# One matmul with doubled rows for the last 64 keys of a head, instead of two half-empty ones

## The chip, the cores and the metric

The kernel runs on one core of one Trainium2 chip. The number that counts is the device time of one execution in microseconds (us). The core has five engines, each with its own queue of instructions: PE (matrix multiply), DVE (vector), ACT (scalar and activation), POOL (GpSimd) and SP, which here only issues DMAs.

## The reference

All inputs are fp32. An attention with a threshold feeds two dense layers:

```
scores = 0.125 * q @ k.T            # 2 batches, 8 heads, 576 queries and keys, 64 dims
scores = where(scores >= rowmax - tau, scores, -1e9)
attn   = softmax(scores)
x      = (attn @ v), heads side by side          # 1152 tokens x 512
x      = max(x @ w1, x @ w2, x @ w3) @ w_out     # 512 -> 768 -> 512
out    = sum_e p[:, e] * (relu(x @ u1[e]) @ u2[e])   # 4 experts, 512 -> 1024 -> 512
```

The change concerns `attn @ v` alone, and of its 576 keys only the last 64 of each head.

## The kernel before, in words

**Precision.** Every fp32 operand is split into a high part (a copy rounded to the fp32r type that PE multiplies) and a low part (what is left, `x - high`), and PE adds up the products of the parts. For `attn @ v` the stationary operand is a tile of 128 columns, 64 columns of the high and 64 of the low values of one head; the moving operand is the weights, first their high part, then their low part. The two halves of the product's 128 rows are then added (`pvlo`, line 483, and line 485).

**Tiling of the attention.** Heads go in pairs, a "job"; there are 4 jobs for each batch. 576 keys are 4 chunks of 128 (`NC = 4`) and a remainder of 64 (`REM`). The queries of a pair are worked in steps: 4 chunks of 128 for each head, and one step for the 64 remaining queries of both heads (`st.h is None`), 9 steps in a job. A step forms scores on PE (`qk`, line 361), the row maximum on DVE (`peak`, 372), the exponential on ACT (`power`, 379), threshold and sum on DVE (`weigh`, 384), the scaling by one over the sum on POOL (`norm`, 391), the transposes on PE (`turn`, 401 and 404), and the split into high and low weights (`cut_hi`, `cut_lo`, 426 to 459).

**The remaining keys.** Both heads of a pair share one tile: head 0's 64 remaining keys are in partitions 0 to 63, head 1's in 64 to 127, so that one transpose (line 404, after every step of head 1 and after the step of the remaining queries) and one copy and one subtraction on all 128 partitions (`ar`, lines 438 and 459) serve both heads. The values `VR` hold zeros in the other head's partitions (the memset of line 292). For each head `gather` (line 474 on) then multiplies 4 chunks with high weights, the remainder with high weights, 4 chunks with low weights and the remainder with low weights: 10 matmuls, of 256 or of 320 columns.

**Stages.** In stage A the four jobs of batch 0 run alone; the order of its instructions on each engine comes from a list scheduler (`ORDER_A = ""`). In stage B the four jobs of batch 1 run between the matmuls of the dense layers for batch 0, and the order on PE, DVE, ACT and POOL is the order in which the program is written (`ORDER_B = "pdas"`). The issue order of SP's DMAs is the scheduler's in both. A third stage, without attention, works the dense layers for the rest of the tokens; its matmuls and those of stage B have line 1190. Their weights are split by ACT (line 711) and POOL (line 715), which the attention uses too.

**Loads.** Remaining values come with one DMA for a job (`vnrem`, line 175), on SP's queue in stage A and on ACT's queue in stage B. The stacked keys and queries that `qk` reads are made by DMAs from one part of the on-chip memory to another on SP's queue (`K`, lines 227 to 230, `QS`, line 243).

Of the kernel before, what the change touches and what calls it, by code (L numbers as in the profile page):

```python
# [22 lines left out]
def fused_kernel(ctx: ExitStack, tc: tile.TileContext, q, k, v, tau, w1, w2, w3, w_out, probs, m_w1, m_w2, out):  # L23
    nc = tc.nc
    B, H, S, D = q.shape
    NT, DM = out.shape
    DFF = w1.shape[1]
    E, _, F2 = m_w1.shape
    P = 128
    NPAIR = H // 2  # L30
    NC = S // P
    MAIN = NC * P
    REM = S - MAIN
# [61 lines left out]
    ident = cst.tile([P, P], F32, name="ident")  # L95
# [39 lines left out]
    at = {}  # L135
# [9 lines left out]
    def atile(shape, dt, tag):  # L145
        return at["pool"].tile(shape, dt, tag=tag, name=tag, bufs=at["bufs"].get(tag, 1))
# [4 lines left out]
    def load_job(job, names="qkv"):  # L151
        b, p = job.b, job.p
        for nm, src in (("q", q), ("k", k), ("v", v)):
            if nm not in names:
                continue
            heads = src[b, 2 * p:2 * p + 2]
            load = nc.scalar.dma_start if nm == "v" and b else nc.sync.dma_start
            main = heads[:, 0:MAIN, :].rearrange("h (p c) d -> p h c d", c=NC)
            if nm == "v":
                t = atile([P, 2, NC, D], F32, "vnat")  # L160
                load(out=t, in_=main)
            else:
                t = atile([P, NC, 2, D], F32, f"{nm}nat")
                for h in range(2):
                    nc.sync.dma_start(out=t[:, :, h, :], in_=main[:, h])
            if nm == "q":
                r = diagonal
                for h in range(2):
                    last = nc.sync.dma_start(out=r[h * REM:(h + 1) * REM, h * D:(h + 1) * D], in_=heads[h, MAIN:S, :])
            elif nm == "k":  # L170
                r = atile([REM, 2, D], F32, "knrem")
                last = nc.sync.dma_start(out=r, in_=heads[:, MAIN:S, :].rearrange("h r d -> r h d"))
            else:
                r = atile([P, D], F32, "vnrem")
                last = load(out=r, in_=heads[:, MAIN:S, :])
            job.raw[nm] = (t, r)
        return last

# [108 lines left out]

    def values(job, follower=None):
        V = atile([P, 2, NC, 2 * D], F32R, "V")
        if job.b == 0 or job.p == 0:  # L290
            at["VR"] = atile([P, 2, 2 * D], F32R, "VR")
            nc.gpsimd.memset(f32(at["VR"]), 0.0)
        VR = at["VR"]
        job.v = (V, VR)
        vt, vr = job.raw["v"]
        vn = vt
        nc.scalar.activation(out=V[:, :, :, 0:D], in_=vn, func=AF.Copy)
        yield
        nc.gpsimd.tensor_tensor(out=V[:, :, :, D:2 * D], in0=vn, in1=f32(V[:, :, :, 0:D]), op=ALU.subtract)
        rows = [slice(h * REM, (h + 1) * REM) for h in range(2)]  # L300
        for h, r in enumerate(rows):
            nc.scalar.activation(out=VR[r, h, 0:D], in_=vr[r, :], func=AF.Copy)
        yield
        for h, r in enumerate(rows):
            nc.gpsimd.tensor_tensor(out=VR[r, h, D:2 * D], in0=vr[r, :], in1=f32(VR[r, h, 0:D]), op=ALU.subtract)
        if follower:
            for _ in range(3):
                yield
            load_job(follower, "v")
# [77 lines left out]
    def norm(st, swift=False):  # L387
        em = views(st)[1]
        su, re = st.stat["sum"], st.stat["r"]
        nc.vector.reciprocal(out=re, in_=su)  # L390
        last = (nc.vector if swift else nc.gpsimd).tensor_scalar(out=em, in0=em, scalar1=re, scalar2=one, op0=ALU.mult, op1=ALU.mult)  # L391
        if st.h is None:
            nc.gpsimd.tensor_scalar(
                out=st.em[:, S:S + REM], in0=st.em[:, MAIN:S], scalar1=1.0, scalar2=1.0, op0=ALU.mult, op1=ALU.mult)
        return last

    def turn(st):
        st.t = ptile_at("T", [P, NC, P])
        off = (st.h or 0) * W
        for j in range(NC):  # L400
            last = nc.tensor.transpose(st.t[:, j, :], st.em[:, off + j * P:off + (j + 1) * P], ident)  # L401
        if st.h != 0:
            st.tm = ptile_at("U", [P, P])
            last = nc.tensor.transpose(st.tm, st.em[:, MAIN:MAIN + 2 * REM], ident)  # L404
        return last

    def pieces(st):
        grp = st.grp
        cols = slice(grp.nn, grp.n) if st.h is None else slice(st.ci * P, (st.ci + 1) * P)
        outs = []  # L410
        for h in range(2):
            if st.h in (h, None):
                if grp.am[h] is None:
                    grp.am[h] = [atile([P, NC, grp.n], F32R, "am") for _ in "hl"]
                src = slice(h * REM, (h + 1) * REM) if st.h is None else slice(0, P)
                outs.append((src, *(x[:, :, cols] for x in grp.am[h])))
        return cols, outs

    def rem_rows(st):
        if st.h == 0:  # L420
            return []
        return [slice(0, P)] if st.h == 1 else [slice(h * REM, (h + 1) * REM) for h in range(2)]

    def cut_hi(st, mode):

        st.mode = mode
        grp = st.grp
        cols, outs = pieces(st)
        if mode == "pool":
            st.copy = atile([P, NC, P], F32, "tcopy")  # L430
            nc.scalar.activation(out=st.copy, in_=st.t, func=AF.Copy)
        else:
            for src, hi, lo in outs:
                nc.scalar.activation(out=hi, in_=st.t[:, :, src], func=AF.Copy)  # L434
        for r in rem_rows(st):
            if not hasattr(grp, "ar"):
                grp.ar = [atile([P, grp.n], F32R, "ar") for _ in "hl"]
            nc.scalar.activation(out=grp.ar[0][r, cols], in_=st.tm[r, r], func=AF.Copy)

    def cut_lo(st):  # L440
        grp = st.grp
        cols, outs = pieces(st)
        if st.mode == "pe":
            t2 = ptile_at("T", [P, NC, P])
            off = st.h * W
            for j in range(NC):
                nc.tensor.matmul(
                    t2[:, j, :], lhsT=st.em[:, off + j * P:off + (j + 1) * P], rhs=ident, is_transpose=True, start=j == 0, stop=False)
        for src, hi, lo in outs:
            if st.mode == "pool":  # L450
# [14 lines left out]
    def gather(grp, swift=False):  # L465
# [7 lines left out]
        for h in range(2):  # L473
            pv = ptile_at("U", [P, n])
            terms = []
            for part in range(2):
                terms += [(V[:, h, j, :], grp.am[h][part][:, j, :]) for j in range(NC)]
                terms.append((VR[:, h, :], grp.ar[part]))
            for i, (l, r) in enumerate(terms):
                at["valued"] = nc.tensor.matmul(pv, lhsT=l, rhs=r, start=i == 0, stop=i == len(terms) - 1)  # L480
            yield
            lo = atile([D, n], F32, "pvlo")
            nc.scalar.activation(out=lo, in_=pv[D:2 * D], func=AF.Copy)
            yield
            nc.vector.tensor_tensor(out=x32[h * D:(h + 1) * D], in0=pv[0:D], in1=lo, op=ALU.add)
            yield
# [850 lines left out]
```

## Time and profile before

| | us |
|---|---|
| median of 3 runs | 713.69 (713.09 to 714.32) |
| the profiled execution | 714.93 |
| its span, from the first to the last instruction | 713.1 |
| busy in the span: PE | 692.1 (97%) |
| DVE | 467.0 (65%) |
| ACT | 360.1 (51%) |
| POOL | 495.9 (70%) |

The shares are averages over three stages that have different limits, so they are read stage by stage below. The records of PE's matmuls have modelled ends that reach into the next matmul; what one of them costs the engine is the distance from one start to the next, not its length. The granted clock of PE was 0.997 of full speed over the span.

### The profile page before, as it was taken

What the parts mean: (1) busy time and instruction counts of PE and PEld (TensorE: products, weight loads), DVE (VectorE), ACT (ScalarE), POOL (GpSimd) and SP (SyncE); (2) the same over time, 40 slices, a digit from 0 to 9 for tenths busy, and PEclk for the clock granted to TensorE, in tenths of its full rate; (3) what the DMA queues carried; (4) which work ended last, traced back from release to release, by engine and by line L of the source; (5) the groups of instructions that cost most, each with busy time, mean ns of one, the idle gap of its engine ahead of it and who ended that gap; (6) DMA issues with size and microseconds to landing.
All of it is one profiled execution on the core that took longest, in us unless ns stands there. A gap on an engine that the chain in (4) does not pass through costs nothing.

```text
span 713.1 us, 11878 instructions
## 1 busy us (share of the span) xinstructions
PE 692.1 (97%) x3961; PEld 612.8 (86%) x3961; DVE 467.0 (65%) x1048; ACT 360.1 (51%) x760; POOL 495.9 (70%) x577
## 2 busy tenths in 40 slices
PE   7899999999999999999999999999999999999997
PEld 6778988877778888888878889999998998998996
DVE  5999898875566676676676467874744644643653
ACT  5788875554555465464555344446524433434430
POOL 4769876786675665676576577789479669669660
PEclk9999999999999999999999999999999999999999
DMA  6863506987868368375333554444122222222103
GB/s 173 190 148 74 161 1 192 272 239 236 239 192 216 112 155 215 101 167 154 119 104 101 185 161 146 148 152 130 60 89 62 87 88 90 83 67 90 57 1 74
DMA packets 108176, 95.04 MB, mean 133 GB/s; under 512 B 26708, under 2 KB 91220, under 8 KB 108116
## 3 DMA queue, kind: packets, MB, share of 16 engines
q1 hardware_dynamic: 91498, 83.24, 41.1%
q10 hardware_dynamic: 16586, 11.05, 5.4%
q8 instruction: 32, 0.52, 0.3%
q14 instruction: 28, 0.23, 0.1%
q0 software_dynamic: 32, 0.00, 0.0%
HBM read 68.96 MB, written 13.37 MB: 115 GB/s over the span
## 4 chain that ended last, share of the span: by engine, by line
PE 82%; POOL 6%; ACT 4%; issue 3%; DVE 3%; DMA 2%; SPq 0%; ACTq 0%; POOLq 0%; DVEq 0%
PE ps L1190 67%; PE u L480 5%; PE s L361 4%; PE t L401 3%; POOL a L715 1%; ACT em L379 1%; DMA krem<-in_k_dram 1%; DVE em L384 1%; POOL em L391 1%; DVE st_negm L372 1%; POOL sl L975 1%; ACT am L434 1%; POOL bt L877 0%; DMA K<-KN 0%; PE u L404 0%
## 5 line engine op out<-in xcount | busy, mean ns | idle before, releaser
L1190 PE MATMUL ps<-b,hh 128*128 128x512 f32 (+1 forms) x584 | 184.7, 390 | 0.0
L715 POOL TENSOR_TENSOR b<-raw,b 128x512 fp32r<-128x512 f32 x64 | 83.1, 1305 | 69.6 <-ACT b L711 69.4
L1190 PEld LDWEIGHTS ps<-b,hh 128*128 128x128 f32 x584 | 108.4, 188 | 20.8
L1190 PE MATMUL ps<-b,hl 128*128 128x512 f32 (+1 forms) x292 | 114.2, 391 | 0.0
L715 POOL TENSOR_TENSOR a<-raw,a 128x512 fp32r<-128x512 f32 (+1 forms) x58 | 72.7, 1255 | 38.8 <-ACT a L711 38.3
L1154 DVE SCALAR_TENSOR_TENSOR acc<-ps,pr,acc 128x512 f32<-128x512 f32 (+1 forms) x64 | 47.4, 741 | 73.8 <-PE ps L1190 73.8
L391 POOL TENSOR_SCALAR em<-em,st_r,one 128x576 f32<-128x576 f32 x70 | 57.6, 823 | 43.6 <-DVE st_r L390 37.0
L379 ACT ACTIVATE em<-s,st_negm 128x576 f32<-128x576 f32 x72 | 53.6, 744 | 64.7 <-DVE st_negm L372 62.4
L1190 PE MATMUL ps<-y0h,a 128*128 128x512 f32 x256 | 84.0, 400 | 0.0
L372 DVE TENSOR_REDUCE st_negm<-s 128x1 f32<-128x576 f32 x72 | 54.2, 754 | 38.9 <-PE s L361 38.4
L1190 PE MATMUL ps<-bt,sh 128*128 128x320 f32 x300 | 69.9, 309 | 0.0
L384 DVE SCALAR_TENSOR_TENSOR em<-s,st_thr,em 128x576 f32<-128x576 f32 x72 | 58.5, 813 | 9.9 <-ACT em L379 7.2
L975 POOL TENSOR_TENSOR sl<-s,sh 128x512 fp32r<-128x512 f32 x50 | 64.7, 1315 | 0.0
L1190 PEld LDWEIGHTS ps<-b,hl 128*128 128x128 f32 x292 | 55.0, 188 | 10.3
L711 ACT ACTIVATE a<-raw 128x512 fp32r<-128x512 f32 (+1 forms) x66 | 39.6, 605 | 37.8 <-DVE raw L755 12.0
L962 POOL TENSOR_TENSOR dl<-wraw,dh 128x512 fp32r<-128x512 f32 (+1 forms) x50 | 50.0, 1021 | 12.2 <-ACT dh L957 8.2
L1081 ACT ACTIVATE hh<-ps 128x320 fp32r<-128x320 f32 x64 | 27.4, 438 | 54.9 <-DVE ps L1008 54.9
L1190 PEld LDWEIGHTS ps<-y0h,a 128*128 128x128 f32 x256 | 47.4, 189 | 8.6
L1190 PE MATMUL ps<-y0l,a 128*128 128x512 f32 x128 | 51.4, 401 | 0.0
L1190 PEld LDWEIGHTS ps<-bt,sh 128*128 128x128 f32 x300 | 51.1, 188 | 0.0
L361 PE MATMUL s<-K,QS 128*128 128x288 f32 x264 | 48.2, 305 | 2.3 <-DVE em L384 1.3
L401 PE MATMUL t<-ident,em 128*128 128x128 f32 x288 | 43.3, 274 | 4.8 <-POOL em L391 3.9
(217 smaller groups left out, 1721.7 us busy)
## 6 DMA issues: line engine op xcount, KB each, us to landing
raw<-in_moe_w_dram SPq DMA_DIRECT2D x96, 256.0 KB
words<-in_moe_w_dram SPq DMA_DIRECT2D x18, 512.0 KB
wraw<-in_moe_w_dram SPq DMA_DIRECT2D x16, 512.0 KB
kept_w<-raw SPq DMA_DIRECT2D x18, 256.0 KB
wraw<-kept_w SPq DMA_DIRECT2D x9, 512.0 KB
K<-KN SPq DMA_DIRECT2D x14, 288.0 KB
K<-KN SPq DMA_DIRECT2D x14, 256.0 KB
sraw<-kept_w ACTq DMA_DIRECT2D x14, 256.0 KB
```

The costliest lines, as they stand in the source:

```text
L361: st.whole = nc.tensor.matmul(st.s[:, kh, 0:HS], lhsT=l, rhs=r, start=i == 0, stop=i == len(terms) - 1)
L372: nc.vector.tensor_reduce(out=st.stat["negm"], in_=views(st)[0], op=ALU.max, axis=AX.XY, negate=True)
L379: return nc.scalar.activation(out=ev, in_=sv, func=AF.Exp, bias=st.stat["negm"])
L384: nc.vector.scalar_tensor_tensor(out=ev, in0=sv, scalar=st.stat["thr"], in1=ev, op0=ALU.is_ge, op1=ALU.mult, accum_out=st.stat["sum"])
L391: last = (nc.vector if swift else nc.gpsimd).tensor_scalar(out=em, in0=em, scalar1=re, scalar2=one, op0=ALU.mult, op1=ALU.mult)
L401: last = nc.tensor.transpose(st.t[:, j, :], st.em[:, off + j * P:off + (j + 1) * P], ident)
L711: nc.scalar.activation(out=b["hi"], in_=b["raw"], func=AF.Copy)
L715: nc.gpsimd.tensor_tensor(out=b["lo"], in0=b["raw"], in1=f32(b["hi"]), op=ALU.subtract)
L962: nc.gpsimd.tensor_tensor(out=rows(b["dl"], x), in0=src, in1=f32(rows(b["dh"], x)), op=ALU.subtract)
L975: nc.gpsimd.tensor_tensor(out=rows(b["sl"], slice(x, x + 2)), in0=rows(b["s"], slice(x, x + 2)), in1=f32(rows(b["sh"], slice(x, x + 2))), ...
L1154: nc.vector.scalar_tensor_tensor(out=accs[t][:, cols], in0=ps, scalar=pe, in1=accs[t][:, cols], op0=ALU.mult, op1=ALU.add)
L1190: nc.tensor.matmul(banks[x], lhsT=l, rhs=r, start=i == 0, stop=i == count - 1)
```

## The change

Both batches are listed in `TWOFOLD`. For these, the moving tile of a head's remaining keys has the high weights in 64 partitions and the low weights in the other 64, `VR` has the same 64 values in both halves, and one matmul does what two did.

- `gather` issues 9 matmuls for a head instead of 10, and the remainder comes last.
- `cut_hi` and `cut_lo` in a step of head 1 work 64 partitions at a time: two copies and two subtractions instead of one each. The subtraction of head 0 reads partitions 0 to 63 and writes 64 to 127, that of head 1 the other way round. In the step of the remaining queries one instruction of 64 x 2 x 64 takes the place of two of 64 x 64.
- In that step POOL no longer copies the 64 columns a second time (line 393), and the transpose has 64 output rows.
- `vnrem` is loaded twice, once into each half, with two DMAs; `VR` is split with one copy and one subtraction on 128 partitions in place of two each on 64, and is not cleared any more.

```
-        if job.b == 0 or job.p == 0:
+        if job.b == 0 or job.p == 0 or twofold:
             at["VR"] = atile([P, 2, 2 * D], F32R, "VR")
-            nc.gpsimd.memset(f32(at["VR"]), 0.0)
+            if not twofold:
+                nc.gpsimd.memset(f32(at["VR"]), 0.0)
...
+                if b in TWOFOLD:
+                    for h in range(2):
+                        last = load(out=r[h * REM:(h + 1) * REM], in_=heads[:, MAIN:S, :].rearrange("h r d -> r h d"))
...
+        parts = [(slice(0, P), slice(0, 2))] if twofold else [(slice(h * REM, (h + 1) * REM), slice(h, h + 1)) for h in range(2)]
+        for r, h in parts:
+            nc.scalar.activation(out=VR[r, h, 0:D], in_=vr[r], func=AF.Copy)
...
-        if st.h is None:
+        if st.h is None and st.grp.job.b not in TWOFOLD:
             nc.gpsimd.tensor_scalar(
                 out=st.em[:, S:S + REM], in0=st.em[:, MAIN:S], scalar1=1.0, scalar2=1.0, op0=ALU.mult, op1=ALU.mult)
...
+            rows = REM if st.h is None and st.grp.job.b in TWOFOLD else P
+            last = nc.tensor.transpose(st.tm[0:rows], st.em[:, MAIN:MAIN + rows], ident)
...
+        if not hasattr(grp, "ar"):
+            grp.ar = atile([P, 2, grp.n], F32R, "ar")
+        if st.h is None:
+            return [(st.tm[0:REM].rearrange("p (h r) -> p h r", h=2), *(grp.ar[r, :, cols] for r in halves))]
+        return [(st.tm[halves[h]], grp.ar[halves[h], h, cols], grp.ar[halves[1 - h], h, cols]) for h in range(2)]
...
+        for tm, hi, lo in rem_rows(st):
+            nc.scalar.activation(out=hi, in_=tm, func=AF.Copy)
...
+        for tm, hi, lo in rem_rows(st):
+            nc.vector.tensor_tensor(out=lo, in0=tm, in1=f32(hi), op=ALU.subtract)
...
             for part in range(2):
                 terms += [(V[:, h, j, :], grp.am[h][part][:, j, :]) for j in range(NC)]
-                terms.append((VR[:, h, :], grp.ar[part]))
+                if b not in TWOFOLD:
+                    terms.append((VR[:, h, :], grp.ar[part]))
+                elif part:
+                    terms.append((VR[:, h, :], grp.ar[:, h, :]))
```

The buffers of `ar` are halved in number and doubled in size.

DVE, near the end of stage A, before (`ar` are the remaining keys' weights, `am` those of the chunks, `em` the exponentials, `x` the product):

```order
L459 TENSOR_TENSOR ar<-u,ar 128x128
L375 TENSOR_SCALAR st_thr<-st_negm,ntau 128x1
L391 TENSOR_SCALAR em<-em,st_r,one 128x576
L384 SCALAR_TENSOR_TENSOR em,st_sum<-s,st_thr,em 128x576
L390 RECIPROCAL st_r<-st_sum 128x1
L391 TENSOR_SCALAR em<-em,st_r,one 128x576
L457 TENSOR_TENSOR am<-t,am 128x4x64
L459 TENSOR_TENSOR ar<-u,ar 64x64 x2
L457 TENSOR_TENSOR am<-t,am 128x4x64
L485 TENSOR_TENSOR x_1647<-u,pvlo 64x256
```

The same place of DVE, after:

```order
L477 TENSOR_TENSOR ar<-u,ar 64x128 x2
L382 TENSOR_SCALAR st_thr<-st_negm,ntau 128x1
L398 TENSOR_SCALAR em<-em,st_r,one 128x576
L391 SCALAR_TENSOR_TENSOR em,st_sum<-s,st_thr,em 128x576
L397 RECIPROCAL st_r<-st_sum 128x1
L398 TENSOR_SCALAR em<-em,st_r,one 128x576
L475 TENSOR_TENSOR am<-t,am 128x4x64
L477 TENSOR_TENSOR ar<-u,ar 64x2x64
L475 TENSOR_TENSOR am<-t,am 128x4x64
L506 TENSOR_TENSOR x_1639<-u,pvlo 64x256
```

Each 128x128 subtraction has become two of 64x128, and the two of 64x64 have become one; what stands around them is the same here.

PE, the first gather of stage B for one head, between matmuls of the dense layers (`ps`), before:

```order
L361 MATMUL s<-K_2721,QS 128x288 x4
L480 MATMUL u<-am,V 128x320 x4
L480 MATMUL u<-ar,VR 128x320
L480 MATMUL u<-am,V 128x320 x4
L480 MATMUL u<-ar,VR 128x320
L1190 MATMUL ps<-b,hh 128x512
```

The same place of PE, after:

```order
L368 MATMUL s<-K_2710,QS 128x288 x4
L501 MATMUL u<-am,V 128x320 x8
L501 MATMUL u<-ar,VR 128x320
L1211 MATMUL ps<-b,hh 128x512
```

One of ten matmuls has gone, and the other with `ar` stands behind all that read `am`.

SP's queue at the start of stage B (`raw` are weights of the dense layers, `knrem` the remaining keys of the next job), before:

```order
L719 DMA raw<-in_moe_w_dram 128x512 x2
L172 DMA knrem<-in_k_dram 64x2x64
L719 DMA raw<-in_moe_w_dram 128x512
L230 DMA K_2721<-KN 64x2x512
L227 DMA K_2721<-KN 64x2x576 x2
L229 DMA K_2721<-KN 64x2x64 x2
L230 DMA K_2721<-KN 64x2x512
L243 DMA QS<-knat 64x512
L243 DMA QS<-qnat 64x512
```

The same place of SP's queue, after:

```order
L740 DMA raw<-in_moe_w_dram 128x512 x3
L235 DMA K_2710<-KN 64x2x512 x2
L232 DMA K_2710<-KN 64x2x576 x2
L234 DMA K_2710<-KN 64x2x64 x2
L248 DMA QS<-knat 64x512
L248 DMA QS<-qnat 64x512
```

The load of `knrem` has gone from the front of the stacked keys to a place behind the next weights, and the second `K` of 64x2x512 stands ahead of the others instead of behind them.

## Rows read from the trace of the kernel before

**Rows 1.** Busy us (count) of PE, PEld, DVE, ACT, POOL by stage; clock, DMA, GB/s.
```profile
14.00:106.00 92.00, 85.45 (x621) 76.24 (x620) 85.37 (x249) 75.38 (x167) 75.91 (x100) 1.00 0.46 115
165.00:402.00 237.00, 233.13 (x1241) 197.01 (x1241) 151.44 (x346) 120.82 (x245) 153.99 (x200) 1.00 0.58 157
402.00:713.00 311.00, 306.08 (x1780) 283.03 (x1778) 177.99 (x359) 125.64 (x277) 218.39 (x213) 1.00 0.32 98
```

**Rows 2.** Chain that ended last, stage B: start, length, what.
```profile
221.89 1.47 PE u L480 x10
...
244.77 1.19 PE u L480 x10
```

**Rows 3.** What DVE waited for in stage A: total, times, longest.
```profile
DVE st_negm L372 <- PE s L361: 2.3, 5, 0.9
DVE em L384 <- ACT em L379: 1.7, 4, 0.6
```

**Rows 4.** DVE in order of time, stage A: start, length, instruction, idle before.
```profile
85.04 0.08 DVE L384 DVE_READ_ACCUMULATOR em<-s,st_thr,em 128x1 f32 x1
85.15 0.48 DVE L485 TENSOR_TENSOR x<-u,pvlo 64x320 f32<-64x320 f32 x1
85.67 0.76 DVE L372 TENSOR_REDUCE st_negm<-s 128x1 f32<-128x576 f32 x1
...
86.41 0.27 DVE L459 TENSOR_TENSOR ar<-u,ar 128x128 fp32r<-128x128 f32 x1
86.60 0.75 DVE L372 TENSOR_REDUCE st_negm<-s 128x1 f32<-128x576 f32 x1
...
102.44 0.44 DVE L459 TENSOR_TENSOR ar<-u,ar 64x64 fp32r<-64x64 f32 x2
102.92 0.42 DVE L457 TENSOR_TENSOR am<-t,am 128x256 fp32r<-128x256 f32 x1
```

**Rows 5.** ACT in order of time, stage A.
```profile
85.62 0.28 ACT L438 ACTIVATE ar<-u 128x128 fp32r<-128x128 f32 x1
85.79 0.41 ACT L495 ACTIVATE x0h<-x 128x256 fp32r<-128x256 f32 x1
...
101.56 0.45 ACT L438 ACTIVATE ar<-u 64x64 fp32r<-64x64 f32 x2 [0.35 <-PE u L404]
102.03 0.60 ACT L431 ACTIVATE tcopy<-t 128x512 f32<-128x512 f32 x1
```

**Rows 6.** PE where it waited in stage B; idle time in brackets.
```profile
195.71 0.65 PE L401 MATMUL t<-ident,em 128*128 128x128 f32 x4 [0.79 <-POOL em L391]
...
202.07 0.66 PE L401 MATMUL t<-ident,em 128*128 128x128 f32 x4 [1.12 <-POOL em L391]
...
366.46 0.55 PE L401 MATMUL t<-ident,em 128*128 128x128 f32 x3 [1.63 <-POOL em L391]
```

**Rows 7.** POOL in order of time, before the second and the third of these waits.
```profile
195.74 0.24 POOL L393 TENSOR_SCALAR em<-em 128x64 f32<-128x64 f32 x1
...
196.19 0.46 POOL L907 TENSOR_TENSOR hmax<-sraw 128x128 f32<-128x128 f32 x1
...
199.54 0.71 POOL L305 TENSOR_TENSOR VR<-vnrem,VR 64x64 fp32r<-64x64 f32 x2
200.34 0.46 POOL L907 TENSOR_TENSOR hmax<-sraw 128x128 f32<-128x128 f32 x1
...
362.15 0.72 POOL L305 TENSOR_TENSOR VR<-vnrem,VR 64x64 fp32r<-64x64 f32 x2
```

**Rows 8.** SP's queue in order of time, start of stage B.
```profile
179.89 0.65 SPq L172 DMA_DIRECT2D knrem<-in_k_dram  x1
...
186.30 0.61 SPq L230 DMA_DIRECT2D K<-KN  x1
...
189.88 0.55 SPq L719 DMA_DIRECT2D raw<-in_moe_w_dram  x1
```

**Rows 9.** ACT's queue, issues of the remaining values in stage B: min/median/max ns.
```profile
L175 ACTq DMA_DIRECT2D vnrem<-in_v_dram x4: 561/571/591, 171.1 to 311.5; - x4
```

More of the change, by code (lines that the diff above doesn't have):

```diff
@@ L72, in fused_kernel @@
     STACKED = 10000
+    TWOFOLD = (0, 1)
     AHEAD_A, LOAD_B, PREP_B = 6, 1, 3
@@ L173, in load_job @@
             else:
-                r = atile([P, D], F32, "vnrem")
-                last = load(out=r, in_=heads[:, MAIN:S, :])
+                r = atile([P, 1 + (b in TWOFOLD), D], F32, "vnrem")
+                if b in TWOFOLD:
+                    for h in range(2):
+                        last = load(out=r[h * REM:(h + 1) * REM], in_=heads[:, MAIN:S, :].rearrange("h r d -> r h d"))
+                else:
+                    last = load(out=r[:, 0, :], in_=heads[:, MAIN:S, :])
             job.raw[nm] = (t, r)
@@ L289, in values @@
         V = atile([P, 2, NC, 2 * D], F32R, "V")
-        if job.b == 0 or job.p == 0:
+        twofold = job.b in TWOFOLD
+        if job.b == 0 or job.p == 0 or twofold:
             at["VR"] = atile([P, 2, 2 * D], F32R, "VR")
-            nc.gpsimd.memset(f32(at["VR"]), 0.0)
+            if not twofold:
+                nc.gpsimd.memset(f32(at["VR"]), 0.0)
         VR = at["VR"]
@@ L299, in values @@
         nc.gpsimd.tensor_tensor(out=V[:, :, :, D:2 * D], in0=vn, in1=f32(V[:, :, :, 0:D]), op=ALU.subtract)
-        rows = [slice(h * REM, (h + 1) * REM) for h in range(2)]
-        for h, r in enumerate(rows):
-            nc.scalar.activation(out=VR[r, h, 0:D], in_=vr[r, :], func=AF.Copy)
+        parts = [(slice(0, P), slice(0, 2))] if twofold else [(slice(h * REM, (h + 1) * REM), slice(h, h + 1)) for h in range(2)]
+        for r, h in parts:
+            nc.scalar.activation(out=VR[r, h, 0:D], in_=vr[r], func=AF.Copy)
         yield
-        for h, r in enumerate(rows):
-            nc.gpsimd.tensor_tensor(out=VR[r, h, D:2 * D], in0=vr[r, :], in1=f32(VR[r, h, 0:D]), op=ALU.subtract)
+        for r, h in parts:
+            nc.gpsimd.tensor_tensor(out=VR[r, h, D:2 * D], in0=vr[r], in1=f32(VR[r, h, 0:D]), op=ALU.subtract)
         if follower:
@@ L403, in turn @@
             st.tm = ptile_at("U", [P, P])
-            last = nc.tensor.transpose(st.tm, st.em[:, MAIN:MAIN + 2 * REM], ident)
+            rows = REM if st.h is None and st.grp.job.b in TWOFOLD else P
+            last = nc.tensor.transpose(st.tm[0:rows], st.em[:, MAIN:MAIN + rows], ident)
         return last
@@ L421, in rem_rows @@
             return []
-        return [slice(0, P)] if st.h == 1 else [slice(h * REM, (h + 1) * REM) for h in range(2)]
+        grp = st.grp
+        cols = pieces(st)[0]
+        halves = [slice(h * REM, (h + 1) * REM) for h in range(2)]
+        if grp.job.b not in TWOFOLD:
+            if not hasattr(grp, "ar"):
+                grp.ar = [atile([P, grp.n], F32R, "ar") for _ in "hl"]
+            return [(st.tm[r, r], grp.ar[0][r, cols], grp.ar[1][r, cols]) for r in ([slice(0, P)] if st.h == 1 else halves)]
+        if not hasattr(grp, "ar"):
+            grp.ar = atile([P, 2, grp.n], F32R, "ar")
+        if st.h is None:
+            return [(st.tm[0:REM].rearrange("p (h r) -> p h r", h=2), *(grp.ar[r, :, cols] for r in halves))]
+        return [(st.tm[halves[h]], grp.ar[halves[h], h, cols], grp.ar[halves[1 - h], h, cols]) for h in range(2)]
     def cut_hi(st, mode):
@@ L434, in cut_hi @@
                 nc.scalar.activation(out=hi, in_=st.t[:, :, src], func=AF.Copy)
[L435 to L438, printed above, removed]
+        for tm, hi, lo in rem_rows(st):
+            nc.scalar.activation(out=hi, in_=tm, func=AF.Copy)
     def cut_lo(st):
@@ L457, in cut_lo @@
                 nc.vector.tensor_tensor(out=lo, in0=st.t[:, :, src], in1=f32(hi), op=ALU.subtract)
-        for r in rem_rows(st):
-            nc.vector.tensor_tensor(out=grp.ar[1][r, cols], in0=st.tm[r, r], in1=f32(grp.ar[0][r, cols]), op=ALU.subtract)
+        for tm, hi, lo in rem_rows(st):
+            nc.vector.tensor_tensor(out=lo, in0=tm, in1=f32(hi), op=ALU.subtract)
     def cut_late(st):
@@ L1223, in fused_kernel @@
     first, rest = ([Job(b, p) for p in range(NPAIR)] for b in range(B))
-    bufs_a = {"K12": 2, "QS": 2, "V": 2, "VR": 2, "em": 3, "am": 6, "ar": 4}
-    bufs_b = {"sraw": 2, "K12": 2, "QS": 2, "em": 2, "am": 4, "ar": 2}
+    bufs_a = {"K12": 2, "QS": 2, "V": 2, "VR": 2, "em": 3, "am": 6, "ar": 2}
+    bufs_b = {"sraw": 2, "K12": 2, "QS": 2, "em": 2, "am": 4, "ar": 1}
     for bf in (bufs_a, bufs_b):
```

## The prediction

> **What bounds the kernel now.** I read the busy time by stage first. In stage A (14 to 106 us) no engine is idle for long, but DVE is the fullest by what it really holds: 85.37 of 92 us [rows 1]. PE shows as much, yet its records reach into the next matmul, so PE has more room than it shows. In stage B (165 to 402) PE is busy 233.13 of 237 us and DVE only 151.44; after 402 PE is busy 306.08 of 311 [rows 1]. So a matmul less is time gained in B, and the gain is carried to the end, because the stage behind is PE's as well. In A an instruction more on DVE is what has to be priced.
>
> Then the waits. In A, DVE's idle time is 92 - 85.37 = 6.6 us, of which 4.0 are waits for scores from PE (2.3) and for the exponential from ACT (1.7) [rows 3]; the rest are gaps between dependent instructions, which nothing fills. In B, PE waited for POOL's scaling at three places: 0.79, 1.12 and 1.63 us [rows 6]. Last the order of time around these places, for the start-to-start distances.
>
> **PE.** Ten matmuls of 320 columns took 1.47 us of the chain and ten of 256 took 1.19 [rows 2]: 0.147 and 0.119 for one. Each job loses two of either kind, 0.53 us, and four jobs lose 2.1 us, in A and again in B. In B this is on the path. In A it only shortens what DVE waits for. That the last term of a gather now needs the low weights of every step costs nothing extra, since low weights were already needed by the tenth matmul.
>
> **DVE in A.** Each of 16 steps of head 1 (four chunks, four jobs) has two subtractions of 64x128 for one of 128x128. A half has as many elements in a partition as the whole, and its length comes out the same: from 0.22 us for each 64x64 to 0.48 for 64x320 it is 0.26 for 256 elements, so 64x128 takes about 0.28, an estimate from these rows; the whole tile took 0.27 [rows 4]. Today the whole costs only 0.19, from 86.41 to the next start at 86.60, since it overlaps its neighbours by 0.08. The halves will not overlap. The row at 85.15 adds in partitions 0 to 63 and writes 64 to 127, as the new subtraction of head 0 does: it starts 0.03 after the end of the row before (85.04 + 0.08), and the next starts 0.04 after its own end. The pair of 64x64 at 102.44, whose second half lies in the other partitions, shows it too: 0.44 for two, and the next 0.04 later.
>
> [...]
>
> So a pair: 0.08 of overlap lost and 0.03 of gap ahead, 0.28, 0.02, 0.28, 0.03, together 0.72 us, which is 0.53 more than 0.19. Sixteen make 8.5 us. The four steps of the remaining queries go from 0.48 us (102.44 to 102.92 [rows 4]) to 0.11 + 0.28 + 0.03 = 0.42, and give back 0.2. DVE gets 8.3 us more work in A.
>
> [...]
>
> How much of 8.3 us lengthens A? If all idle time of DVE could be used, 8.3 - 6.6 = 1.7; if none, 8.3. I take half of the 4.0 us of waits as filled, since PE hands scores over earlier but ACT gets busier, and price A at +6.3 us.
>
> **ACT and POOL in A.** ACT's copy has 0.17 us from start to start today (85.62 to 85.79); the second half and what follows it will not overlap either, as 101.56 to 102.03 shows for a pair (0.47) [rows 5]. A pair of 64x128 is 0.28 + 0.01 + 0.28 + 0.02 = 0.59, 0.42 more, 6.7 us for 16. The remaining queries give back 4 x 0.30, and the copies of `VR`, priced alike, another 4 x 0.30. ACT gets 4.3 us on 75.38 of 92, and stays below DVE. POOL loses the second copy, the memsets and half of the `VR` work: it is relieved, and does not set the pace. SP issues one DMA more for each job, of the shape of `knrem` (0.65 [rows 8]); the values are loaded a job ahead and the stacked keys queue behind them, so I take nothing, and 2.6 us if that cover is missing.
>
> **Stage B beside PE's 2.1 us.** The second wait (1.12) stands behind a stretch of POOL without a pause. From it go line 393 and the memset behind it, 195.74 to 196.19 = 0.45 us, and the pair of line 305, 199.54 to 200.34 = 0.80, becomes one instruction of 128 elements, for which I take the 0.46 of the 128x128 one behind it [rows 7]. That is 0.79 us less, and 0.33 is left of the wait. The pair of line 305 comes again at 362.15 [rows 7], ahead of the third wait: 0.34 less. The first wait (0.79) goes back to weights whose DMA was issued at 189.88, behind SP's whole row of stacked keys [rows 8]. `knrem` (0.65) now stands behind it, and one `K` of 0.61 moves from its end to its front, where SP may be waiting for a free buffer anyway. I take 0.66 of the 1.26; bounds 0 and 0.79. Both add up, since the second wait begins where the first ends.
>
> In B the longer pairs on DVE (16 x 0.53) and ACT lie in idle time: DVE has 85 us of it. A second DMA for `vnrem` holds ACT's queue another 0.57 us for each job [rows 9], ahead of weight copies that POOL waits for; PE uses these much later. Without that cover it is 2.3 us. I take nothing.
>
> B: -2.1 - 0.66 - 0.79 - 0.34 = -3.9 us; between -2.1 and -4.0 without a new wait.
>
> **Sum.** +6.3 - 3.9 = +2.4 us. The profiled execution took 714.93 us (span 713.1 and 1.8 around it) and would take 717.3; it was 1.2 us above the median of the runs. On the median of 713.69 the forecast is 716.1 us.
>
> **Rivals.**
> 1. Stage A takes up the new work (faster). The scheduler puts the halves where DVE waits, and with PE 2.1 and POOL some 3 us lighter (4 x 0.79) the waits go: A grows by the 1.7 us bound, total 1.7 - 3.9 = -2.2, 711.5 us. It decides as soon as A grows by less than 2.5. For it: four engines share A, so DVE's waits depend on others that get lighter. Against it: much of DVE's idle time is gaps.
> 2. A half costs its length and no overlap: 16 x 0.28 less 0.2 is 4.3 us, 2.0 of it filled, total 2.3 - 3.9 = -1.6, 712.1 us. The row at 85.15 speaks against it. [...]
> 3. It cancels out: all 4.0 us of waits are filled, A grows by 4.3, total +0.4, 714.1 us.
> 4. Nothing is filled and B gains only its matmuls, because a DMA or the longer ACT work makes POOL late again: 8.3 - 2.1 = +6.2, 719.9 us.
>
> That the matmuls don't go away is no rival: the order shows nine where ten were.
>
> **How the numbers follow.** Forecast 0.45; rivals 0.15, 0.06, 0.22 and 0.12. A measurement of this kernel can tell a change from none at about 0.2%, 1.4 us: faster is below 712.3, slower above 715.1. Slower: 0.41 of the forecast's 0.45, all of rival 4, 0.03 of rival 3, together 0.56. Faster: rivals 1 and 2 and 0.03 of rival 3, 0.24. No change: the other 0.20. Cases of both signs hold much of the chance: the forecast's own range is 714 to 718, and the range for 8 in 10 reaches from just below rival 1 to just short of rival 4, 711.4 to 719.3.
>
> **What will show it.** In the profile after, `ar` on DVE should take 0.6 us and more from the first half's start to the next instruction, with gaps in place of overlaps, and DVE should be busy about 93 us between the start of the attention and the first long row of layer matmuls, which should begin some 6 us later. The wait at 202 should shrink to about 0.3 us, the one at 196 nearly vanish, and the third lose 0.3; the distance from the first to the last gather of batch 1 should shrink by its matmuls and that third wait. If A has kept its length, the price of the halves or the share that is filled was wrong; if B has not become shorter by 2 us, PE did not pace it.

## The result and the profile after

The changed kernel took 719.57 us (median of 4 runs, 717.70 to 721.20), the kernel before 713.68 in the same comparison. The ratio is 1.0075, 95% interval 1.006 to 1.009: 5.4 us slower (4.3 to 6.4), where 2.4 was forecast. By the ratio, 713.69 us become 719.0, just inside the stated range of 711.4 to 719.3; the median itself lies 0.3 above it. The direction and the bill for stage A were right; stage B gave back far less than the forecast took. Three single executions of the runs below that were far slower than all others (one each of `after_raw5`, `b_late` and the kernel before) are in none of the ratios.

The profiled execution took 717.7 us (span 715.8), the fastest of the four. Busy time by stage, with the columns of [rows 1]:

```profile
14.00:106.00 92.00, 80.14 (x571) 69.97 (x570) 87.30 (x249) 74.95 (x167) 70.29 (x87) 1.00 0.45 113
165.00:402.00 237.00, 231.84 (x1220) 194.34 (x1219) 159.42 (x361) 125.40 (x255) 154.16 (x195) 1.00 0.60 162
```

DVE is now all but full in stage A, while PE and POOL have become emptier; in stage B, DVE got 8 us more work and PE did not get busier.

The pairs, DVE and then ACT in order of time in stage A (start, length of the group, instruction; they answer to [rows 4, 5]):

```profile
41.61 0.09 DVE L391 DVE_READ_ACCUMULATOR em<-s,st_thr,em 128x1 f32 x1
41.73 0.59 DVE L477 TENSOR_TENSOR ar<-u,ar 64x128 fp32r<-64x128 f32 x2
42.35 0.21 DVE L382 TENSOR_SCALAR st_thr<-st_negm,ntau 128x1 f32<-128x1 f32 x1
```

```profile
40.45 0.57 ACT L456 ACTIVATE ar<-u 64x128 fp32r<-64x128 f32 x2
41.04 0.69 ACT L241 ACTIVATE QNh<-u,qscale 128x512 fp32r<-128x512 f32 x1
```

A pair holds DVE from 41.73 to 42.35 = 0.62 us, starts 0.03 behind the end of the row before it (41.61 + 0.09), and with the 0.08 of overlap that is lost there it costs 0.73; the forecast said 0.72. ACT's takes 0.59 from start to start, as forecast. DVE's waits in stage A (total, times, longest; [rows 3]):

```profile
DVE ar L477 <- ACT ar L456: 0.9, 2, 0.6
DVE em L391 <- ACT em L386: 0.5, 2, 0.2
DVE st_negm L379 <- PE s L368: 0.4, 1, 0.4
```

The 4.0 us of waits for scores and exponentials have shrunk to 0.9, and 0.9 for the new pairs have come.

How long stage A is, I read from two of PE's rows: the scores of the third step and the last `ar` matmul of batch 0. What lies ahead of them differs between executions of one program: the third step began at 29.89 and 29.13 us in two later kernels (`b_only`, `halves_b`) whose stage A is that of before, and at 30.07 in one (`after_raw5`) whose stage A is that of the changed kernel. Kernels with the same stage A agree in the distance to 0.1 us. It holds 14 of the 16 steps of head 1; two lie ahead of it. Before, then after:

```profile
30.21 0.70 PE L361 MATMUL s<-K,QS 128*128 128x288 f32 x4
...
107.56 0.31 PE L480 MATMUL u<-ar,VR 128*128 128x320 f32 x1
```

```profile
28.62 0.69 PE L368 MATMUL s<-K,QS 128*128 128x288 f32 x4
...
110.92 0.31 PE L501 MATMUL u<-ar,VR 128*128 128x320 f32 x1
```

77.35 us became 82.30: stage A is 4.95 us longer. That the span grew by only 2.7 (713.1 to 715.8) is this execution's early start: 1.6 us at the third step. Busy time in this stretch, before and after:

```profile
30.21:107.56 77.35, 72.38 (x523) 64.80 (x522) 71.47 (x209) 64.26 (x146) 62.91 (x85) 1.00 0.39 99
28.62:110.92 82.30, 71.88 (x509) 62.85 (x508) 77.54 (x220) 67.21 (x153) 61.76 (x77) 1.00 0.37 95
```

Stage B, the chain that ended last ([rows 2]):

```profile
225.76 1.32 PE u L501 x9
...
248.35 1.07 PE u L501 x9
```

Nine matmuls instead of ten, 0.15 and 0.12 us less, sixteen times: the 2.1 us that were forecast. But PE's waits in stage B are these (idle time in brackets; [rows 6] had three):

```profile
167.04 0.73 PE L1211 MATMUL ps<-hh,a 128*128 128x512 f32 x2 [0.82 <-POOL a L736]
...
178.75 0.74 PE L1211 MATMUL ps<-y0h,a 128*128 128x512 f32 x2 [0.27 <-POOL a L736]
...
200.53 0.66 PE L408 MATMUL t<-ident,em 128*128 128x128 f32 x4 [1.23 <-POOL em L398]
...
205.94 0.66 PE L408 MATMUL t<-ident,em 128*128 128x128 f32 x4 [0.18 <-POOL em L398]
...
355.18 1.18 PE L501 MATMUL u<-am,V 128*128 128x256 f32 x8 [1.06 <-DVE st_r L397]
...
369.74 0.66 PE L408 MATMUL t<-ident,em 128*128 128x128 f32 x4 [1.15 <-POOL em L398]
```

POOL ahead of the second wait, where `VR` takes one instruction; the second copy and the memset are gone from the rows ahead of it ([rows 7]):

```profile
203.78 0.45 POOL L312 TENSOR_TENSOR VR<-vnrem,VR 128x128 fp32r<-128x128 f32 x1
```

The second wait fell from 1.12 to 0.18 and the third from 1.63 to 1.15, a little more than forecast. The first, which was to shrink by 0.66, grew from 0.79 to 1.23, and a gather at 355 now waits 1.06 us. From the last `ar` matmul of batch 0 to the last of batch 1 it was 401.56 - 107.56 = 294.00 us and is 404.35 - 110.92 = 293.43: stage B gave 0.6 us instead of 3.9.

The first wait, from SP's queue and ACT's row ([rows 8] answers):

```profile
185.80 1.35 SPq L235 DMA_DIRECT2D K<-KN  x2
...
194.59 1.69 SPq L740 DMA_DIRECT2D raw<-in_moe_w_dram  x3
```

```profile
197.67 0.63 ACT L732 ACTIVATE a<-raw 128x512 fp32r<-128x512 f32 x1 [1.97 <-DMA raw<-in_moe_w_dram]
```

From its first `K` on, the row of stacked keys is no shorter: 185.80 to 194.59 = 8.79 us, against 181.26 to 189.88 = 8.62. The `K` that moved to its front gained nothing. That `knrem` has left the front did gain time: the row now begins 0.49 us after DVE has split the keys, before it was 1.17. (Over all profiles it is 0.48 to 0.54 without `knrem` there and 0.35 to 1.30 with it.) But the split keys come later, as ACT's copy of them stands right behind a copy of weights, and ACT waited longer for the load of those. Before, then after:

```profile
178.09 0.63 ACT L711 ACTIVATE a<-raw 128x512 fp32r<-128x512 f32 x1 [2.89 <-DMA raw<-in_moe_w_dram]
179.40 0.69 DVE L211 TENSOR_TENSOR KN<-u,KN 128x512 fp32r<-128x512 f32 x1 [3.48 <-ACT KN L209]
```

```profile
183.35 0.63 ACT L732 ACTIVATE a<-raw 128x512 fp32r<-128x512 f32 x1 [3.72 <-DMA raw<-in_moe_w_dram]
184.62 0.69 DVE L216 TENSOR_TENSOR KN<-u,KN 128x512 fp32r<-128x512 f32 x1 [4.27 <-ACT KN L214]
```

PE reached its transposes 4.38 us later than before (195.71 - 0.79 = 194.92, now 200.53 - 1.23 = 199.30), the split of the keys began 5.22 later: 0.84 lost against PE. Less the 0.68 that the row begins earlier, and with 0.17 for its length and 0.11 for the last load (ACT began 3.08 us after its issue, before 2.97), that is the 0.44 by which the wait has grown. Why the weights ahead of the keys came late was not traced. In `b_only`, with the same queue, the keys lost only 0.12 against PE, and the wait fell to 0.46.

### The profile page after: what moved, and what is told of

The parts are those of the page before. It is cut to its first block, busy times and chain, and to the rows that moved or that the text cites. A ratio compares the mean times of both kernels' runs of the same rounds, so it can differ in the third digit from the quotient of the medians.

```text
span 715.8 us, 11859 instructions
## 1 busy us (share of the span) xinstructions
PE 689.9 (96%) x3929; PEld 608.3 (85%) x3929; DVE 480.5 (67%) x1072; ACT 366.9 (51%) x776; POOL 491.4 (69%) x556
## 4 chain that ended last, share of the span: by engine, by line
PE 74%; DVE 8%; POOL 6%; issue 5%; ACT 5%; DMA 1%; SPq 0%; DVEq 0%; POOLq 0%; ACTq 0%
PE ps L1211 63%; PE u L501 3%; PE s L368 3%; PE t L408 2%; DVE em L391 2%; DVE st_negm L379 2%; POOL a L736 2%; ACT em L386 1%; DVE ar L477 1%; DMA krem<-in_k_dram 1%; POOL em L398 1%; DVE raw L776 1%; POOL sl L996 1%; POOL hl L841 1%; DVE bits L771 1%
## 5 line engine op out<-in xcount | busy, mean ns | idle before, releaser
L368 PEld LDWEIGHTS s<-K,QS 128*128 128x128 f32 x264 | 40.1, 189 | 11.4 <-DVE em L391 3.1
```

Of the source, the lines that this page charges most:

```text
L368: st.whole = nc.tensor.matmul(st.s[:, kh, 0:HS], lhsT=l, rhs=r, start=i == 0, stop=i == len(terms) - 1)
```

## The experiments

Twelve kernels, each timed in 5 rounds against the kernel before, in three comparisons. The column A is the distance from the third step to the last `ar` matmul of batch 0, B the distance from there to the last `ar` matmul of batch 1, both read as above, from one execution each; of `b_late` no profile is read.

| run | median us | ratio to before, 95% interval | A, us | B, us |
|---|---|---|---|---|
| before | 713.7 to 714.7 | | 77.35 | 294.00 |
| the change | 719.57 | 1.0075 (1.006 to 1.009) | 82.30 | 293.43 |
| a_only | 721.01 | 1.0092 (1.0078 to 1.0106) | 82.35 | 296.69 |
| b_only | 712.50 | 0.9971 (0.9959 to 0.9983) | 77.43 | 292.31 |
| halves_a | 717.19 | 1.0033 (1.0022 to 1.0045) | 80.60 | 294.54 |
| cols_a | 716.20 | 1.0022 (1.0012 to 1.0032) | 78.92 | 294.80 |
| acts_a | 717.46 | 1.0041 (1.0029 to 1.0053) | 80.76 | 294.72 |
| acts_cols_a | 716.32 | 1.0026 (1.0014 to 1.0037) | 79.80 | 294.83 |
| halves_b | 715.76 | 1.0020 (1.0010 to 1.0030) | 77.39 | 295.35 |
| after_raw5 | 717.04 | 1.0028 (1.0016 to 1.0041) | 82.35 | 291.66 |
| before_raw5 | 713.72 | 0.9992 (0.9982 to 1.0003) | 77.43 | 293.94 |
| b_raw5 | 711.25 | 0.9953 (0.9937 to 0.9969) | 77.38 | 291.37 |
| b_late | 712.82 | 0.9964 (0.9951 to 0.9977) | | |
| b_late_raw5 | 712.23 | 0.9964 (0.9949 to 0.9978) | 77.38 | 293.94 |

**One batch at a time.** `TWOFOLD = (1,)` and `TWOFOLD = (0,)`, with the buffers of `ar` to match.

> The change in batch 1 alone; batch 0 as before. Theory 1 (stage A pays for the halves, stage B earns): stage B loses its 16 matmuls (2.1 us) and gets part of it back as new waits, as the profile of the change showed (from the first to the last gather of batch 1 it was 1.7 us shorter, and the stretch ahead of the first gather half a us longer): 711.5 to 712.7 us, ratio 0.997 to 0.9985, with the wait of 1.1 us in front of a late gather still there. Rival (the longer pairs on ACT and DVE cost stage B as much as the matmuls give): 713.2 to 714.5, ratio 1.000.

> The change in batch 0 alone; batch 1 as before. Theory 1: stage A carries the whole loss, and more than the whole, since batch 1 no longer gives anything back: the median of the change was 5.9 us above before, so 719 to 721.5 us here, ratio 1.008 to 1.011, and the first long layer matmul begins 4 to 7 us later than before. Rival (half of the loss lies in stage B, which is disturbed whatever stage A does): 716 to 717.5, ratio 1.003 to 1.005.

The times came out as theory 1 had it: batch 1 alone is 2 us faster than before, batch 0 alone 6.6 slower. But not all of that lay in stage A: the profile of `a_only` has 5.0 us more there and 2.7 more in stage B. Batch 1 works there as before, and yet its first wait was the longest of all:

```profile
201.57 0.65 PE L408 MATMUL t<-ident,em 128*128 128x128 f32 x4 [2.42 <-POOL em L398]
```

The load was issued at 194.18 and ACT began at 198.72, 4.54 us later, where the kernel before had 2.97. How long such a load takes to land differs between profiles, from 2.97 to 4.54 us in six of them.

**What stage A pays for.** The kernel before, batch 0, with one instruction of 128x128 split in two: on DVE or on ACT, by partitions or by columns. In short form (`...` stands for what is left out):

```
# halves_a (DVE), acts_a (the same for ACT's copy): partitions 0 to 63, then 64 to 127
-        nc.vector.tensor_tensor(out=grp.ar[1][r, cols], in0=st.tm[r, r], ...)
+        for h in range(2): r = slice(h * REM, (h + 1) * REM)
+            nc.vector.tensor_tensor(out=grp.ar[1][r, cols], in0=st.tm[r, 0:P], ...)
# cols_a (DVE), acts_cols_a (ACT): all partitions, columns 0 to 63, then 64 to 127
```

> The kernel before, with one edit: in batch 0 the subtraction of 128x128 on DVE is done as two of 64x128, on partitions 0 to 63 and 64 to 127. ACT, PE and POOL do what they did. A pair starts in its old overlap, its second half starts 0.01 to 0.03 us behind the end of the first, and what follows 0.03 behind the second: 0.28 + 0.02 + 0.28 + 0.03 = 0.61 us for a pair instead of 0.19, 16 x 0.42 = 6.7 us more work for DVE. Theory 1 (DVE's held halves are what stage A pays for): +3 to +6 us, 717 to 719.5, ratio 1.004 to 1.008. Rival (ACT's halves or the order of the list scheduler are what stage A pays for): within 1 us of before, ratio 0.999 to 1.0015.

> The kernel before, with one edit: in batch 0 the subtraction of 128x128 on DVE is done as two of 128x64, side by side in the columns, so that there are as many instructions as in the run with halves of 64 partitions, but all on partitions 0 to 127. Theory 1 (it is the lost overlap at a change of partitions that costs): each starts in the overlap of the one before, a pair takes 0.25 to 0.30 us instead of 0.19, 1 to 2 us more work for DVE, and the time is 713.5 to 715, ratio 0.9995 to 1.002. Rival (any 16 instructions more on DVE cost as much): as the run with the halves, ratio 1.004 to 1.008.

> The kernel before, with one edit: in batch 0 ACT's copy of 128x128 of the remaining keys' weights is done as two of 64x128. DVE does what it did. 16 pairs, 0.42 us more each, are 6.7 us more work for ACT in stage A. With DVE's halves alone the first layer matmuls came 2.2 to 2.9 us later, with the whole change 3.4 to 4.0. Theory 1 (the other 1.1 us are ACT's halves): +0.5 to +2 us, ratio 1.0007 to 1.003. Rival (ACT has room and its halves cost nothing, the remainder is the order that the list scheduler finds): ratio 0.999 to 1.0007, or, as any new order may cost what the run with 128x64 columns showed (1.0022), a stage A that is longer with DVE's waits for ACT unchanged.

> The kernel before, with one edit: in batch 0 ACT's copy of 128x128 of the remaining keys' weights is done as two of 128x64, so that there are as many instructions as with ACT's halves, but all on partitions 0 to 127. Theory 1 (ACT, like DVE, loses its overlap at a change of partitions, and that is what the halves cost there): a pair takes some 0.3 us from its first start to the next instruction in place of 0.57, and the time is at most 1.5 us above before, ratio 0.999 to 1.002. Rival (16 instructions more on ACT cost as much in any shape, or the order of the list scheduler does): ratio 1.003 to 1.005.

A pair and what follows it, in order of time, in `halves_a`, `cols_a`, `acts_a` and `acts_cols_a`:

```profile
43.62 0.58 DVE L459 TENSOR_TENSOR ar<-u,ar 64x128 fp32r<-64x128 f32 x2
44.23 0.16 DVE L390 RECIPROCAL st_r<-st_sum 128x1 f32<-128x1 f32 x1
```

```profile
42.74 0.35 DVE L459 TENSOR_TENSOR ar<-u,ar 128x64 fp32r<-128x64 f32 x2
43.00 0.16 DVE L390 RECIPROCAL st_r<-st_sum 128x1 f32<-128x1 f32 x1
```

```profile
50.70 0.54 ACT L438 ACTIVATE ar<-u 64x128 fp32r<-64x128 f32 x2
51.26 0.74 ACT L379 ACTIVATE em<-s,st_negm 128x576 f32<-128x576 f32 x1
```

```profile
50.38 0.35 ACT L438 ACTIVATE ar<-u 128x64 fp32r<-128x64 f32 x2
50.59 0.45 ACT L495 ACTIVATE x0h<-x 128x256 fp32r<-128x256 f32 x1
```

On DVE halves of the partitions take 0.61 us from start to start and halves of the columns 0.26; on ACT 0.56 and 0.21. The instruction count is the same, and halves of the partitions cost 0.35 us a pair more on either engine. Not all of it is the change of partitions, since a half of 64x128 has twice the columns of one of 128x64. The pairs of 64x64, which have as many columns as 128x64 and do change partitions, took 0.48 us on DVE and 0.47 on ACT [rows 4, 5]: of the 0.35 us, 0.22 and 0.26 go with the change of partitions, and the other 0.13 and 0.09 with the length.

Stage A does not follow these prices one to one. DVE's halves lengthen it by 3.25 us, ACT's by 3.41, both with the rest of the change by 4.95: they are not a sum. In `acts_a`, where DVE does what it did, DVE waited 3.8 us for the exponential, before 1.7 [rows 3]:

```profile
DVE em L384 <- ACT em L379: 3.8, 8, 0.7
```

So ACT's longer pairs reach DVE as waits. The columns lengthen the stretch by 1.57 and 2.45, though its 14 pairs add only 14 x 0.07 = 1.0 us on DVE and 14 x 0.04 = 0.6 on ACT (0.26 against the 0.19 of [rows 4], 0.21 against the 0.17 of [rows 5]). The list scheduler found another order of stage A for each of these kernels; what of 1.57 and 2.45, and so of 3.25 and 3.41, is due to that order, no run separates. So of theory 1 the price per pair stands, but not what stage A makes of it: `halves_a` came out just below its ratio of 1.004, `cols_a` just above its 1.002, `acts_a` above its 1.003, and `acts_cols_a` lies between its two expectations, with an interval that overlaps that of `acts_a`.

**The late gather in stage B.** The kernel before, in batch 1, with ACT's copy and DVE's subtraction both in halves of 64 partitions (as above, `grp.job.b == 1`); ten matmuls as before.

> The kernel before, with one edit: in batch 1 the copy of 128x128 on ACT and the subtraction of 128x128 on DVE are both done as two of 64x128; ten matmuls for each gather, as before. Theory 1 (in stage B ACT and DVE wait for each other in their written order, so a pair's 0.42 us on ACT and 0.42 on DVE add up to some 0.8 us before the next row maximum, and reach PE where it has less room than that): a new wait of 0.7 to 1.1 us before the second gather of a head pair at about 351 us, where there are 0.05 us in the kernel before; +0.7 to +1.5 us in all, ratio 1.001 to 1.002. Rival (they lie in idle time, as the prediction had it, and that wait comes from the nine matmuls, which bring PE there earlier): ratio 0.9995 to 1.0005 and a wait below 0.3 us.

```profile
351.61 0.71 PE L480 MATMUL u<-am,V 128*128 128x256 f32 x4 [0.81 <-DVE st_r L390]
```

The wait is there without the nine matmuls, and the kernel is 1.4 us slower (0.7 to 2.1). How it comes about is to be seen in the changed kernel, ACT and then DVE, and in the kernel before, DVE:

```profile
347.40 0.56 ACT L456 ACTIVATE ar<-u 64x128 fp32r<-64x128 f32 x2
347.98 0.60 ACT L1152 ACTIVATE hh<-ps 128x512 fp32r<-128x512 f32 x1
```

```profile
349.99 0.61 DVE L477 TENSOR_TENSOR ar<-u,ar 64x128 fp32r<-64x128 f32 x2
350.63 0.76 DVE L379 TENSOR_REDUCE st_negm<-s 128x1 f32<-128x576 f32 x1
...
354.62 0.41 DVE L506 TENSOR_TENSOR whole<-u,pvlo 64x256 f32<-64x256 f32 x1
```

```profile
346.47 0.28 DVE L459 TENSOR_TENSOR ar<-u,ar 128x128 fp32r<-128x128 f32 x1
346.73 0.76 DVE L372 TENSOR_REDUCE st_negm<-s 128x1 f32<-128x576 f32 x1
```

ACT's pair delays `hh`, a layer's activations; DVE's `hl` needs `hh` and stands ahead of DVE's pair; behind that pair stands the next row maximum, for which ACT's exponential waits. That exponential, and what is written behind it, delays `whole`, which frees the buffer of `u` that the gather needs. The profile names `st_r`, a short instruction behind `whole` on DVE; `whole` ends at 355.03 and the gather starts at 355.18. In the kernel before PE waited 0.05 us there.

> The change in batch 1 alone, and in batch 1 ACT's copies of the remaining keys' weights are written behind the other work that falls due in that step (the copy of a layer's activations, a weight copy), instead of ahead of it. PE's order is the same as with the change in batch 1 alone. Theory 1 (the wait of 1.06 us before the late gather is the sum of ACT's and DVE's longer pairs): ACT's 0.55 us leave the chain, the wait falls to 0.4 to 0.6 us, the time by some 0.5 us to 711.5 to 712.5, ratio 0.996 to 0.997. Rival (DVE's pair alone sets it, or the copies then come too late for DVE): the wait stays at 1 us or more, ratio 0.997 to 0.998.

> As the run before it in this list (the change in batch 1 alone, NR 5, NB 9), and with ACT's copies of the remaining keys' weights behind the work that falls due in that step. Theory 1 (the 1.06 us before the late gather are ACT's and DVE's longer pairs in a row): that wait falls to 0.4 to 0.6 us and the time by 0.5 us against the run without it, ratio 0.9945 to 0.996. Rival (DVE's pair alone sets the wait, or the copies then come too late for DVE): a wait of 1 us or more there, no gain.

```
-        for tm, hi, lo in rem_rows(st):            # in cut_hi
+        for tm, hi, lo in [] if grp.job.b else rem_rows(st):
         ...
         for tm, hi, lo in rem_rows(st):            # in cut_lo
+            grp.job.b and nc.scalar.activation(out=hi, in_=tm, func=AF.Copy)
```

This repair showed no gain. The ratio of `b_late`, 0.9964, lies where theory 1 had it, but its interval holds the 0.9971 of `b_only` as well; `b_late_raw5`, at the same ratio, is no faster than `b_raw5` (0.9953). PE's waits in `b_late_raw5` say why:

```profile
206.13 0.63 PE L408 MATMUL t<-ident,em 128*128 128x128 f32 x4 [1.50 <-DVE am L475]
...
350.81 1.20 PE L501 MATMUL u<-am,V 128*128 128x256 f32 x8 [0.81 <-DVE st_r L397]
```

Taking ACT's pair out of the chain shortened the gather's wait from 1.06 to 0.81 us only, less than theory 1 had, and a wait of 1.50 came up at 206, behind a copy of ACT that started at 204.67 (202.29 in `b_raw5`). Why ACT is later there was not traced.

**The first wait.** One buffer more for the layers' fp32 weights, one less for their split parts:

```
-    NR, NA, NB = 4, 6, 10
+    NR, NA, NB = 5, 6, 9
```

> The changed kernel with one buffer of the layers' fp32 weights more (NR 4 to 5) and one of their split parts less (NB 10 to 9). On PE, DVE, ACT and POOL the order of instructions is the same; on SP's queue one load of weights more stands ahead of the row of stacked keys at the start of stage B. Theory 1 (PE's wait at the first transposes of batch 1, 1.23 us after the change and 2.42 with the change in batch 0 alone, is for weights whose load stands behind that row, and its landing time is what makes the executions differ): the wait falls below 0.4 us, the time to 716.5 to 718.5 us, ratio to the kernel before 1.003 to 1.006 in place of 1.0075, and the executions differ by less. Rival (that wait comes from the work of POOL and ACT around it): wait and time stay, ratio 1.007 to 1.009.

> The kernel before with one buffer of fp32 weights more and one of split parts less (NR 5, NB 9), the control for the same edit on the changed kernel, which brought that one from 1.0075 to 1.0028 of before and took away its wait at the first transposes of batch 1. Theory 1 (in the kernel before that wait is 0.79 us, so the buffer is worth that and the rest of the 2.5 us belongs to the change, whose longer stage A shifts this row of loads against the matmuls): the wait at 196 us vanishes, ratio 0.998 to 0.9995. Rival (the buffer is worth the same in every kernel): ratio 0.995 to 0.997.

> The change in batch 1 alone, with NR 5 and NB 9. Theory 1 (what is left of the first wait, 0.46 us in front of the first transposes of batch 1, goes, and at most 0.2 us of the second): 711.3 to 712.3 us, ratio 0.995 to 0.9965. Rival (the loads moved ahead on SP's queue hold up the stacked keys, or the buffer taken from the split parts is missed later): ratio 0.997 to 0.999.

With the changed kernel, SP's queue and PE at the first transposes of batch 1:

```profile
180.44 5.81 SPq L740 DMA_DIRECT2D raw<-in_moe_w_dram  x6
186.34 1.34 SPq L235 DMA_DIRECT2D K<-KN  x2
```

```profile
200.08 0.60 PE L408 MATMUL t<-ident,em 128*128 128x128 f32 x4
```

Six loads stand ahead of the row in place of five, and the wait of 1.23 us is gone: it was for the load behind the stacked keys. The ratio fell from 1.0075 to 1.0028, a little below what theory 1 had; the two come from two comparisons, but their intervals do not overlap. That is 3.4 us, more than the one wait, and stage B of its profile is 1.8 us shorter than the changed kernel's; what else the buffer saves was not told apart. The spread of its executions, which theory 1 expected to shrink, did not (714.62 to 718.33 us, before 717.70 to 721.20). In the kernel before, the buffer is worth nothing that can be measured, and the wait, which theory 1 expected to vanish, only fell from 0.79 to 0.58:

```profile
194.47 0.66 PE L401 MATMUL t<-ident,em 128*128 128x128 f32 x4 [0.58 <-POOL em L391]
```

So the buffer pays together with the change, not by itself. `b_raw5`, the change in batch 1 alone with that buffer, is the fastest of all: 0.9953, 3.4 us below the kernel before. Its interval overlaps that of `b_only` (0.9971), so the buffer's own share there is not settled. Its wait before the late gather is still there:

```profile
348.19 1.18 PE L501 MATMUL u<-am,V 128*128 128x256 f32 x8 [1.06 <-DVE st_r L397]
```

## Why the prediction was right and wrong, step by step

- **Price of a pair:** right, 0.73 for 0.72 us on DVE, 0.59 for 0.59 on ACT. Rival 2 falls with it.
- **How much of it stage A pays:** right, as far as it can be read: 4.95 us for 6.3, over a stretch with 14 of the 16 pairs. For 14 pairs the forecast's sum is 14 x 0.53 - 0.2 - 2.0 = 5.2. DVE's busy time in the stretch grew by 6.1 us (71.47 to 77.54) and its idle time shrank by 1.1. Its waits for scores and exponentials fell by 3.1 and 0.9 of new waits came: 2.2 of 4.0 were filled, about the half that was taken, while the gaps around the pairs added idle time. What the two pairs ahead of the stretch cost is hidden by a start that differs by 1.6 us. The first layer matmuls begin 4.0 us later (101.28, now 105.24), 5.5 when the early start is taken out.
- **"ACT ... stays below DVE":** by the busy time it does, but that it therefore costs nothing was wrong. ACT's halves alone, with the order that the scheduler found for them, lengthen stage A by 3.41 us (`acts_a`). In stage A of the kernel before, DVE waited 1.7 us for ACT's exponential [rows 3] and ACT 3.6 us for DVE's row maximum, and ACT, 82% busy (75.38 of 92 us [rows 1]), was not off the path.
- **Stage B's matmuls, the second and the third wait:** right: 2.1, 0.94 and 0.48 us, for 2.1, 0.79 and 0.34.
- **The first wait:** wrong, +0.44 for -0.66. Between these two profiles `knrem` brought what it was to bring (0.68 for 0.65) and the `K` that moved nothing, but the split keys, which the forecast took as fixed against PE, came 0.84 us later behind a wait for weights. And what ends last there is the landing of a load: from its issue to ACT's start it took 2.97 to 4.54 us in six of these profiles (before, the change, `a_only`, `b_only`, `halves_a`, `cols_a`).
- **"In B the longer pairs ... lie in idle time":** the step that failed. DVE does have idle time in stage B, 77.6 us of 237 after the change, but ACT and DVE work in a written order in which each waits for the other (ACT 55.2 us for row maxima, DVE 12.0 for `hh` and 6.0 for exponentials), and their longer pairs came one behind the other before a row maximum. PE lost 1.06 us at one gather; `halves_b` shows 0.81 with the pairs alone.
- **The second DMA for `vnrem` in stage B, "I take nothing":** wrong at one of the four jobs, by a small amount. Its two issues hold ACT's queue for 1.37 us where one held it for 0.56 [rows 9], and ACT goes on 0.05 us behind them, with `y0h` and then the weight copies that POOL waits for:

```profile
174.79 1.37 ACTq L178 DMA_DIRECT2D vnrem<-in_v_dram  x2
176.21 0.60 ACT L868 ACTIVATE y0h<-ps 128x512 fp32r<-128x512 f32 x1 [1.36 <-PE ps L1211]
```

  The profile names PE, but `y0h` starts the same 0.05 us behind the two issues in `b_only`, `after_raw5` and `b_raw5` too. PE's wait for those weights, 0.27 us at 179, stands in all five profiles with the change in batch 1 (0.27 to 0.47) and at this place in none without it. PE's wait at 167, 0.82 us where it was 0.48 before, lies ahead of these DMAs; `acts_a`, with one DMA for a job in stage B, has 0.82 there too. Its cause was not tested.

Of the 5.4 us, the profiled execution explains 5.0 in stage A less 0.6 in stage B. The remaining 1 us stays open, as a second profile of the changed kernel was not taken. The two pairs ahead of the stretch may be in it, and so may the spread of executions, for which the first wait, 0.46 to 2.42 us in the profiles without the extra buffer, is a candidate. The time is that of rival 4, but with another split: stage A did fill waits, and stage B lost even part of what its matmuls gave.

## What to carry to other kernels

Where two engines feed each other in a fixed order, price a longer instruction along the loop through both, not by either engine's idle time: DVE had 85 us of that in stage B, and PE lost 1.06 us at one gather all the same. An instruction split by partitions can cost three times what the whole did (0.61 for 0.19 us), one split by columns little more than the whole (0.26): look up the start-to-start distance in the trace before trading such a split for a matmul. And a change that pays in the stage that PE bounds should be made there alone, as the kernel's own switch by batch allows (0.9971 of before in `b_only`, 1.0075 with both batches).

## What the runs showed of the hardware

- ACT, too, lost its overlap where the partitions changed: behind a pair of 64x128 (`acts_a`) the next instruction began 0.02 us after its end, behind a pair of 128x64 (`acts_cols_a`) 0.14 before it; on DVE it was 0.03 after (`halves_a`) and 0.09 before (`cols_a`). A pair of 64x64 took 0.47 us from start to start on ACT and one of 128x64, with as many columns, 0.21. On DVE it was 0.48 and 0.26.
- ACT's own work stood behind the DMA issues on its queue: at the first job of stage B one issue took 0.56 us in the kernel before and two took 1.37 in the changed kernel, and in both the next activation began 0.05 us behind them.
- In one execution a lower granted clock came behind a wait. PE stood idle for 2.42 us in `a_only` and worked from 201.57 us on. The granted clock was 1.00 from 196 to 202.8 us, 0.52 from 202.8 to 206 and 0.97 from 206 to 212:

```profile
202.80:206.00 3.20, 3.20 (x9) 2.49 (x9) 1.50 (x5) 1.49 (x5) 3.12 (x5) 0.52 0.80 233
```

Matmuls of 512 columns then started 0.43 us apart instead of 0.23: seven or eight of them, some 1.5 us more. After the wait of 1.23 us in the changed kernel's profile the granted clock stayed at 1.00 (200.5 to 208 us). Whether the wait brought the lower clock, no run tested.
